# A new timetable for sixteen weight conversions under the attention loop, and shorter zero fills

## The chip, the core and the metric

The kernel runs on one core of a Trainium2 chip. The metric is device time in microseconds (us): the median of three runs is 734.9 us (732.71 to 736.11). The engines are TensorE (PE in the profile, its weight loads PEld), VectorE (DVE), ScalarE (ACT), GpSimd (POOL) and SyncE (SP), which here issues nearly all transfers.

## The reference

Three layers in a row, all in float32 (the last layer's weights arrive as 64-bit floats).

```python
# 1 gated linear attention: q, k, v, f_logit are [4, 8, 768, 48]
f = sigmoid(f_logit)
for t in range(768):
    state = f[t] * state + outer(k[t], v[t])
    y[t] = q[t] @ state
x = y as [3072 tokens, 384]
# 2 mixture of 8 experts, one expert for each token
logits = normed(x) @ normed(expert_emb).T / tau
e = argmax(logits)
x = softmax(logits)[e] * (relu(x @ w1[e]) @ w2[e])      # w1 384x1024, w2 1024x384
# 3 gated layer
out = (((x @ g1) * (x @ g2)) @ w3) @ w_out              # g1, g2 384x1024, w3 1024x1024, w_out 1024x384
```

## The kernel before

**Stages.** Attention is cut into 24 units of 128 time steps (four batches, six chunks of time); a loop of 26 rounds, `for i in range(NU + 2)` at L792, runs them as a software pipeline: in round i the table `parts` (L783) calls each step for unit i minus its own delay. After the loop a hand-written tail ends the routing (which expert takes which token), and the stage of the experts follows, then the last layer. Each token's row is scattered by its rank into `xsd`, 3072 rows of room for each expert; an expert later reads a fixed number of rows (up to 448), so rows that no token fills must hold zeros.

**Conversions.** The last layer's weights come as 64-bit floats. While attention runs, class `Early` (L238) turns sixteen pieces into float32: pieces 0 to 7 are `w_out` (128 rows of 384), 8 to 15 the first four row tiles of `w3` in halves (128 rows of 512). A piece in round u passes `words` (ACT, two reads of `raw`, L263 and L264), `bits` (DVE, L269 and L270), one round later `sums` (POOL, L276), and for `w_out` also `upper` (ACT, L283) and `lower` (POOL, L288). `self.at` (L246) says which round takes which piece: six pieces in seven rounds, in rounds 6 to 11, 13 to 18 and 20 to 23. A piece of `w_out` is 384 KB on its way, one of `w3` 512 KB.

**Loads.** At the end of round i SP is handed the loads of `f_logit` for unit i + 3, of k and q for i + 2 and of v for i (L806 to L809), then a piece's load into one of three `raw` buffers (L810): in round 4 the first three, later always piece k + 3 at the end of the round after piece k's. In rounds 2, 3, 5, 6, 7, 9, 10 and 11 a zero fill of `xsd` follows (L823): rows LO = 256 to 448 of one expert's room. SP takes its list in order, and each transfer waits for the eighth transfer before it.

**Order on the engines.** The schedule is manual: each engine executes in the order in which the calls stand. On ACT `words` stands after the copy of `xl` (L533) and before the copy of `y` (`yT`, L490); a late piece therefore holds up `yT`, whose PSUM bank the transpose `kb` (L466) of the next round takes on TensorE.

**The flag.** `finish_route` (L666) ends with a flag: 1 if an expert's tokens do not fit its window, or if the forget gates are too small. With the flag set, a slow general path is executed after the rest.

Of the kernel before, what the change touches and what calls it, by code (L numbers as in the profile page):

```python
# [7 lines left out]
F32 = mybir.dt.float32  # L8
# [4 lines left out]
ALU = mybir.AluOpType  # L13
AX = mybir.AxisListType
# [5 lines left out]
def attn_moe_glu_kernel(  # L20
# [16 lines left out]
    nc = tc.nc  # L37
    PE, V, A, G, SP = nc.tensor, nc.vector, nc.scalar, nc.gpsimd, nc.sync
# [3 lines left out]
    P = 128  # L42
    NP = H // 2
    NC = S // P
    NU = N // P
# [5 lines left out]
    DENSE = N + CAP  # L51


    LO = 256

    const = ctx.enter_context(tc.tile_pool(name="const", bufs=1))
    dram = ctx.enter_context(tc.tile_pool(name="dram", bufs=1, space=DRAM))
# [2 lines left out]
    def bank(shape, name, tag="ps"):  # L60
        acc = tag == "acc"
        return psum[acc].tile(shape, F32, tag="acc" if acc else "ps", name=name)
# [3 lines left out]
    ones = const.tile([P, P], BF16, name="ones")  # L66
# [11 lines left out]
    flag = const.tile([P, 1], I32, name="flag")  # L78
# [22 lines left out]
    early = pre_pool.enter_context(tc.tile_pool(name="early", side="right", bufs=1, reuse_waits="tile"))  # L101
# [11 lines left out]
        return t.bitcast(F32)  # L113

    RY, RW, RL = 2, 2, 1
    GAP_TILES, BG0, RAW = 4, 6, 3
    FILL = (2, 3, 5, 6, 7, 9, 10, 11)
    PASSES = ((0, 0), (0, 1), (1, 0))

    class Background:  # L120
        def __init__(self):
            self.q = []
# [112 lines left out]
    def w3_piece(i, c):  # L235
        return g3[i * P:(i + 1) * P, c * 512:(c + 1) * 512], 512, "g3", to_w3(i, c)

    class Early:  # L238
# [4 lines left out]
        def __init__(self):  # L243
            self.src = [(go[j * P:(j + 1) * P, :], DM, j) for j in range(KF)]
            self.src += [w3_piece(i, c)[0:2] + ((i, c),) for i in range(GAP_TILES) for c in range(2)]
            self.at = {BG0 + k + k // 6: k for k in range(len(self.src))}  # L246
            self.raw, self.t, self.z = {}, {}, {}

        def load(self, k):
# [154 lines left out]
    fl = lambda t: t.rearrange("p a b -> p (a b)")  # L404

    def s_pre(u):
        for hs in (slice(H // 2, H), slice(0, H // 2)) if u == 0 else (slice(0, H),):
            f = fs[u % NB][:, hs, 0:D]
            A.activation(out=f, in_=f, func=AF.Tanh, scale=0.5)
            if u == 0:  # L410
                A.activation(out=f, in_=f, func=AF.Identity, scale=0.5, bias=half[:, 0:1])
            else:
                G.tensor_scalar(out=f, in0=f, scalar1=0.5, scalar2=0.5, op0=ALU.mult, op1=ALU.add)
# [130 lines left out]
    rt = attn.enter_context(tc.tile_pool(name="rt", reuse_waits="tile", bufs=1))  # L544
# [98 lines left out]
    def choose():  # L643


        b = bank([P, E], "lead", "acc")
        PE.matmul(out=b, lhsT=ones, rhs=base)
        yield
        key, hot, t = [rt.tile([P, E], F32, name=n) for n in ("lkey", "lhot", "lt")]
        s = rt.tile([P, 2], F32, name="ls")  # L650
        V.scalar_tensor_tensor(out=key, in0=b, scalar=float(E), in1=numc, op0=ALU.mult, op1=ALU.subtract)
        yield
        V.tensor_reduce(out=s[:, 0:1], in_=key, axis=AX.X, op=ALU.max)
        yield
        V.tensor_scalar(out=hot, in0=key, scalar1=s[:, 0:1], scalar2=None, op0=ALU.is_equal)
        yield
        V.tensor_tensor(out=t, in0=hot, in1=num, op=ALU.mult)
        V.tensor_scalar(out=hot, in0=hot, scalar1=float(2 * E * N), scalar2=None, op0=ALU.mult)
        yield
        V.tensor_reduce(out=s[:, 1:2], in_=t, axis=AX.X, op=ALU.add)  # L660
        V.tensor_tensor(out=numc, in0=num, in1=hot, op=ALU.subtract)
        yield
        V.tensor_copy(out=first[:, 0:1], in_=s[:, 1:2])
        V.tensor_scalar(out=first[:, 1:2], in0=s[:, 1:2], scalar1=float(N), scalar2=None, op0=ALU.mult)

    def finish_route():  # L666
        okb = rt.tile([P, 1], BF16, name="okb")
        low = rt.tile([P, 1], F32, name="low")
        V.tensor_reduce(out=low, in_=pend.rearrange("p u j -> p (u j)"), axis=AX.X, op=ALU.min)
        V.tensor_scalar(out=okb, in0=low, scalar1=1e-18, scalar2=None, op0=ALU.is_ge)  # L670
        yield
        b, b2 = bank([P, E], "cnt", "acc"), bank([P, 1], "ok", "acc")
        PE.matmul(out=b, lhsT=ones, rhs=base)
        PE.matmul(out=b2, lhsT=ones, rhs=okb)
        yield
        cnt, key, rank, cs, ci, inc, sl = [rt.tile([P, E], F32, name=n) for n in ("cnt", "key", "rank", "cs", "ci", "inc", "sl")]
        gt, hot, t = [rt.tile([P, E, E], F32, name=n) for n in ("cgt", "chot", "ct")]
        fl = rt.tile([P, 2], F32, name="fl")
        big = [P, E, E]
        rows = lambda a: a.unsqueeze(1).to_broadcast(big)  # L680
        cols = lambda a: a.unsqueeze(2).to_broadcast(big)
        V.tensor_tensor(out=cnt, in0=b, in1=cbase, op=ALU.subtract)
        yield
        V.tensor_scalar(out=key, in0=cnt, scalar1=float(E), scalar2=None, op0=ALU.mult)
        yield
        V.tensor_tensor(out=key, in0=key, in1=numc, op=ALU.subtract)
        yield
        V.tensor_tensor(out=gt, in0=rows(key), in1=cols(key), op=ALU.is_gt)
        yield
        V.tensor_reduce(out=rank, in_=gt, axis=AX.X, op=ALU.add)  # L690
        yield
        V.tensor_tensor(out=hot, in0=rows(rank), in1=cols(num), op=ALU.is_equal)
        yield
        V.tensor_tensor(out=t, in0=hot, in1=rows(num), op=ALU.mult)
        V.tensor_tensor(out=hot, in0=hot, in1=rows(cnt), op=ALU.mult)
        yield
        V.tensor_reduce(out=sl, in_=t, axis=AX.X, op=ALU.add)
        V.tensor_reduce(out=cs, in_=hot, axis=AX.X, op=ALU.add)
        yield
        V.tensor_copy(out=slot_e, in_=sl)  # L700
        V.tensor_scalar(out=slot_r, in0=sl, scalar1=float(N), scalar2=None, op0=ALU.mult)
        V.tensor_tensor_scan(out=inc, data0=cs, data1=cs, initial=0.0, op0=ALU.add, op1=ALU.bypass)
        V.tensor_tensor(out=ci, in0=cs, in1=win, op=ALU.subtract)
        V.tensor_tensor(out=offs, in0=inc, in1=cs, op=ALU.subtract)
        V.tensor_reduce(out=fl[:, 0:1], in_=ci, axis=AX.X, op=ALU.max)
        V.tensor_scalar(out=fl[:, 1:2], in0=b2, scalar1=P - 0.5, scalar2=None, op0=ALU.is_lt)
        V.tensor_scalar(out=fl[:, 0:1], in0=fl[:, 0:1], scalar1=0.5, scalar2=None, op0=ALU.is_gt)
        V.tensor_tensor(out=flag, in0=fl[:, 0:1], in1=fl[:, 1:2], op=ALU.add)

    groups = {u0 + n - 1: (u0, n) for u0, n in ((0, 6), (6, 6), (12, 4), (16, 4))}  # L710
    with tc.manual_schedule():
# [45 lines left out]
        def pick_heads():  # L757
            for hb in range(2):
                src = ident[:, 64 * hb:64 * hb + D].unsqueeze(1).to_broadcast([P, NP, D])
                G.tensor_copy(out=sel[:, :, D * hb:D * hb + D], in_=src)  # L760
# [9 lines left out]
        cvt = Early()  # L770
# [16 lines left out]
            (s_out, 3), (s_sq, 4), (cvt.upper, 1), (s_uu, 3),  # L787
        )

        pick_heads()  # L790
        s_pre(0)
        for i in range(NU + 2):  # L792
            for part, late_by in parts:
                if late_by is None:
                    part()
                elif 0 <= i - late_by < NU:
                    part(i - late_by)
            if i == NU - 1:
                spread.append(RL)
            if i == NU - 1:  # L800
                routing.append(choose())
            if i == NU:
                SP.dma_start(out=w1s, in_=phase_src(0, 0, SP))
            if i - 4 in groups:
                routing.append(route(*groups[i - 4]))
            load(f_logit, fs, i + 3)  # L806
            load(k, ks, i + 2)
            load(q, qs, i + 2)
            load(v, vs, i)  # L809
            for n in range(RAW) if i == BG0 - 2 else (cvt.at[i - 1] + RAW,) if i - 1 in cvt.at else ():  # L810
                cvt.load(n)
            if i == 4:
                constants()
            if i == 0:
                warm(8)
                zeros()
            if i in (1, 2, 3):
                step(en)
            if i == 8:
                SP.dma_start(out=idd.rearrange("(p c) w -> p (c w)", c=32), in_=zero[0:DENSE // 32, 0, 0:32].bitcast(I32))  # L820
            if i in FILL:
                e = FILL.index(i)
                SP.dma_start(out=xsd[e * N + LO:e * N + CAP, :].rearrange("(p c) w -> p c w", c=4), in_=zero[0:(CAP - LO) // 4])  # L823
            if i == NU or i == NU + 1:
                step(turn_w[i - NU], 2)
# [345 lines left out]
                V.tensor_copy(out=acc, in_=ob)  # L1171
                SP.dma_start(out=out[bass.ds(r0, P), :], in_=acc)

    with tc.If(nc.values_load(flag[0:1, 0:1], min_val=0, max_val=2) != 0):
        general()


# [28 lines left out]
```

## Time and profile before

| | us |
|---|---|
| median of three runs | 734.9 |
| the profiled execution | 737.25 |
| its span, first to last instruction | 735.5 |
| attention rounds (start to about 150) | about 150 |
| routing's tail, up to the first expert's matmul | 181.09 |
| experts, then the last layer | the rest |

The profiled execution is 2.35 us above the median; 1.75 us of it lie around the span. The page's first part gives each engine's busy time: PE 715.9 us (97%), DVE 348.5, ACT 337.1, POOL 339.7. The mean granted TensorE clock is 0.998 of full speed, the level of 2.4 GHz. In a timeline a row is start, duration, engine, line, operation, output and input, the number of instructions merged in it (x), and in brackets the idle time just before it with what ended it.

### The profile page before, as it was taken

How to read it: one execution, taken by the hardware profiler on the slowest of the kernel's cores; microseconds unless marked ns; L12 is line 12 of the kernel's file. 1: busy time of each engine (PE TensorE's matmuls, PEld its weight loads, DVE VectorE, ACT ScalarE, POOL GpSimd, SP SyncE). 2: the span in 40 equal slices, each digit the busy share in tenths (PEclk: the TensorE clock that was granted, in tenths of full speed). 3: DMA queues.
4: the chain of work that ended last, by engine and by line, in shares of the span. 5: the costliest groups of instructions: out<-in, count | busy, mean ns of one | idle time of the engine just before them, and what ended most of it. 6: DMA issues, size and time to landing. Idle time of an engine off the chain costs nothing.

```text
span 735.5 us, 13353 instructions
## 1 busy us (share of the span) xinstructions
PE 715.9 (97%) x5170; PEld 655.9 (89%) x5170; DVE 348.5 (47%) x682; ACT 337.1 (46%) x703; POOL 339.7 (46%) x423
## 2 busy tenths in 40 slices
PE   8999999989999999999999999999999999999995
PEld 7998989879999999999999988988888888888885
DVE  8889899967556464345343132222322322322322
ACT  5687878755667465465554532122112121121210
POOL 5467787784887676584564952202202201221002
PEclk9999999999999999999999999999999999999999
DMA  9999999742866778644443330000100100100001
GB/s 178 224 216 221 231 238 227 179 174 75 275 205 236 214 238 259 190 148 149 134 141 108 90 85 1 31 13 1 43 1 1 43 1 1 43 1 23 21 1 46
DMA packets 132159, 86.50 MB, mean 118 GB/s; under 512 B 106482, under 2 KB 114682, under 8 KB 132090
## 3 DMA queue, kind: packets, MB, share of 16 engines
q1 hardware_dynamic: 128617, 75.34, 37.9%
q0 software_dynamic: 3072, 9.46, 3.4%
q8 instruction: 42, 0.69, 0.4%
q10 hardware_dynamic: 400, 0.79, 0.3%
q14 instruction: 28, 0.22, 0.1%
HBM read 70.57 MB, written 15.01 MB: 116 GB/s over the span
## 4 chain that ended last, share of the span: by engine, by line
PE 59%; issue 9%; DMA 3%; POOL 2%; ACT 1%; SPq 1%; DVE 0%; POOLq 0%; ACTq 0%; DVEq 0%
PE acc L942 12%; PE hb L928 12%; PE pa L1024 11%; PE pb L1024 10%; PE ob L1037 10%; PE wpb L184 3%; DMA stg<-in_moe_w_dram 2%; DMA gd<-gt 1%; PE xb L915 1%; POOL out_dram L1044 1%; PE w3b L173 0%; POOL x L142 0%; POOL gt L229 0%; ACT wh L141 0%; POOL wl L142 0%
## 5 line engine op out<-in xcount | busy, mean ns | idle before, releaser
L142 POOL TENSOR_TENSOR wl<-stg,wh 128x384 fp32r<-128x384 f32 (+1 forms) x119 | 136.3, 1176 | 57.2 <-ACT wh L141 55.4
L1027 DVE TENSOR_TENSOR a<-a,pb 128x512 f32<-128x512 f32 x48 | 33.0, 687 | 182.0 <-PE pb L1024 175.7
L1037 PE MATMUL ob<-wp,ab 128*128 128x384 f32 x576 | 108.4, 339 | 0.1
L1037 PEld LDWEIGHTS ob<-wp,ab 128*128 128x128 f32 x576 | 102.2, 188 | 4.2 <-DVE ab L1030 0.4
L942 PE MATMUL acc<-h,wh 128*128 128x448 f32 (+7 forms) x384 | 104.2, 351 | 1.4 <-ACT h L930 0.7
L928 PE MATMUL hb<-xT,wh 128*128 128x448 f32 (+7 forms) x384 | 102.4, 348 | 0.0
L1024 PE MATMUL pa<-x,wh 128*128 128x512 f32 x288 | 90.2, 394 | 0.0
L1024 PE MATMUL pb<-x,wh 128*128 128x512 f32 x288 | 89.9, 393 | 0.0
L931 DVE SCALAR_TENSOR_TENSOR h<-hb,h 128x448 fp32r<-128x448 f32 (+7 forms) x64 | 37.0, 578 | 106.0 <-ACT h L930 105.8
L1026 ACT COPY a<-pa 128x512 f32<-128x512 f32 x48 | 28.2, 586 | 120.6 <-PE pa L1024 120.6
L1044 POOL DMA_INDIRECT out_dram<-o,didx x24 | 23.2, 965 | 129.7 <-DVE o L1043 126.3
L142 POOL TENSOR_TENSOR x<-xd,x 128x512 fp32r<-128x512 f32 x18 | 22.8, 1290 | 120.3 <-ACT x L141 120.3
L1029 ACT CAST ab<-a 128x512 fp32r<-128x512 f32 x48 | 29.8, 621 | 104.8 <-DVE a L1027 104.8
L141 ACT CAST wh<-stg 128x384 fp32r<-128x384 f32 (+1 forms) x121 | 61.2, 562 | 29.8 <-DMA stg<-in_moe_w_dram 23.6
L942 PEld LDWEIGHTS acc<-h,wh 128*128 128x128 f32 x384 | 70.4, 188 | 4.8 <-DVE h L931 1.9
L928 PEld LDWEIGHTS hb<-xT,wh 128*128 128x128 f32 x384 | 70.8, 188 | 1.3
L928 PE MATMUL hb<-xT,wl 128*128 128x448 f32 (+7 forms) x192 | 66.7, 347 | 0.0
L942 PE MATMUL acc<-h,wl 128*128 128x448 f32 (+7 forms) x192 | 66.6, 347 | 0.0
L1024 PEld LDWEIGHTS pb<-x,wh 128*128 128x128 f32 x288 | 54.2, 188 | 12.7
L1024 PEld LDWEIGHTS pa<-x,wh 128*128 128x128 f32 x288 | 53.6, 188 | 9.2
L930 ACT ACTIVATE h<-hb 128x448 fp32r<-128x448 f32 (+7 forms) x64 | 32.4, 506 | 62.2 <-PE hb L928 62.1
L1024 PE MATMUL pb<-x,wl 128*128 128x512 f32 x144 | 56.9, 395 | 0.0
(200 smaller groups left out, 1280.7 us busy)
## 6 DMA issues: line engine op xcount, KB each, us to landing
stg<-in_moe_w_dram SPq DMA_DIRECT2D x30, 768.0 KB
raw<-in_moe_w_dram SPq DMA_DIRECT2D x28, 512.0 KB
xs<-xsd SPq DMA_DIRECT2D x8, 675.5 KB
q<-in_q_dram SPq DMA_DIRECT2D x24, 192.0 KB
k<-in_k_dram SPq DMA_DIRECT2D x24, 192.0 KB
v<-in_v_dram SPq DMA_DIRECT2D x24, 192.0 KB
f<-in_f_logit_dram SPq DMA_DIRECT2D x23, 192.0 KB
raw<-in_moe_w_out_dram SPq DMA_DIRECT2D x8, 384.0 KB
```

Of the source, the lines that this page charges most:

```text
L141: A.copy(out=hi, in_=src)
L142: eng.tensor_tensor(out=lo, in0=src, in1=f32(hi), op=ALU.subtract)
L928: PE.matmul(out=b, lhsT=w[x][:, kk, cs], rhs=xT[e][y][:, kk, :], start=(kk + n == 0), stop=(kk == KD - 1 and n == 2))
L930: A.activation(out=h[0], in_=b, func=AF.Relu)
L931: V.scalar_tensor_tensor(out=h[1], in0=b, scalar=0.0, in1=f32(h[0]), op0=ALU.max, op1=ALU.subtract)
L942: PE.matmul(out=acc[d], lhsT=w[x][:, s % 4, d * P:(d + 1) * P], rhs=hs[s][y], start=(s + n == 0), stop=(s == KF - 1 and n == 2))
L1024: PE.matmul(out=b, lhsT=w[x][:, kk, cs], rhs=x2[n][y][:, kk, :], start=(kk + m == 0), stop=(kk == KD - 1 and m == 2))
L1026: A.copy(out=t, in_=pa)
L1027: V.tensor_tensor(out=t, in0=t, in1=pb, op=ALU.mult)
L1029: A.copy(out=ab[s][0], in_=t)
L1037: PE.matmul(out=oacc[t], lhsT=ab[s][x][:, t * P:(t + 1) * P], rhs=wp[:, y, s, :], start=(s + m == 0), stop=(s == KF - 1 and m == 2))
L1044: ins = G.indirect_dma_start(out=out, out_offset=bass.IndirectOffsetOnAxis(ap=didx[:, j:j + 1], axis=0), in_=o, in_offset=None,)
```

## The change

Pieces stand in four of every five rounds, 6 to 9, 11 to 14, 16 to 19 and 21 to 24, so the last falls in round 24, after the last unit's round 23. Two loads are issued in round 4, and later piece k + 2 at the end of the round after piece k's: for the third and fourth piece of each group of four that is the round just before its `words`. The number of `raw` buffers stays three. The zero fills begin at row 320, and the flag is set too if an expert has fewer than 320 tokens.

```diff
-    LO = 256
+    LO = 320
-    GAP_TILES, BG0, RAW = 4, 6, 3
+    GAP_TILES, BG0, RAW, AHEAD = 4, 6, 3, 2
-            self.at = {BG0 + k + k // 6: k for k in range(len(self.src))}
+            self.at = {BG0 + k + k // 4: k for k in range(len(self.src))}
-        fl = rt.tile([P, 2], F32, name="fl")
+        fl = rt.tile([P, 4], F32, name="fl")
...
-        V.tensor_tensor(out=flag, in0=fl[:, 0:1], in1=fl[:, 1:2], op=ALU.add)
+        V.tensor_reduce(out=fl[:, 2:3], in_=cs, axis=AX.X, op=ALU.min)
+        V.tensor_scalar(out=fl[:, 2:3], in0=fl[:, 2:3], scalar1=LO - 0.5, scalar2=None, op0=ALU.is_lt)
+        with nc.allow_low_precision(reason="sums of zeros and ones"):
+            V.tensor_reduce(out=flag, in_=fl[:, 0:3], axis=AX.X, op=ALU.add)
...
+        early = (cvt.words, cvt.bits, cvt.sums, cvt.upper, cvt.lower)
...
-                elif 0 <= i - late_by < NU:
+                elif 0 <= i - late_by < (NU + 2 if part in early else NU):
...
-            for n in range(RAW) if i == BG0 - 2 else (cvt.at[i - 1] + RAW,) if i - 1 in cvt.at else ():
+            for n in range(AHEAD) if i == BG0 - 2 else (cvt.at[i - 1] + AHEAD,) if i - 1 in cvt.at else ():
                 cvt.load(n)
...
-    with tc.If(nc.values_load(flag[0:1, 0:1], min_val=0, max_val=2) != 0):
+    with tc.If(nc.values_load(flag[0:1, 0:1], min_val=0, max_val=3) != 0):
```

SP's list at the end of round 7 and through round 8, before (`raw_818` is piece 3, `raw_926` piece 4):

```order
L386 DMA v3_127<-in_v_dram 128x8x48
L253 DMA raw_818<-in_moe2_w_out_dram 128x768
L823 DMA xsd_83<-wp_91 48x1544
L386 DMA f2_123<-in_f_logit_dram 128x8x48
L386 DMA k1_119<-in_k_dram 128x8x48
L386 DMA q1_116<-in_q_dram 128x8x48
L386 DMA v0_124<-in_v_dram 128x8x48
L253 DMA raw_926<-in_moe2_w_out_dram 128x768
```

The same place of SP's list in the changed kernel, where `raw_816` is piece 2 and `raw_924` piece 3:

```order
L387 DMA v3_127<-in_v_dram 128x8x48
L254 DMA raw_816<-in_moe2_w_out_dram 128x768
L829 DMA xsd_83<-wp_91 32x1544
L387 DMA f2_123<-in_f_logit_dram 128x8x48
L387 DMA k1_119<-in_k_dram 128x8x48
L387 DMA q1_116<-in_q_dram 128x8x48
L387 DMA v0_124<-in_v_dram 128x8x48
L254 DMA raw_924<-in_moe2_w_out_dram 128x768
```

The list has the same shape; each of its places holds an earlier piece, and the fills have 32 partitions for 48.

ACT in round 8, changed kernel: the reads of the piece loaded in the list above at the end of round 7 (before, round 8 reads piece 2, `raw_517`, loaded in round 4, and `raw_818` is read in round 9):

```order
L534 COPY xt_142<-xl_865 128x384
L264 ACTIVATE gt_875<-raw_816 128x384
L265 ACTIVATE z_876<-raw_816 128x384
L526 COPY sbd2_130<-scm2_134 64x4x48 x2
L491 COPY yT_906<-y_889 128x512
```

The piece that SP issues at the end of a round is now read in the next one, ahead of `yT`.

POOL around round 25, before (`am` is the last unit's mask, the DMAs are the scatters of tokens):

```order
L634 DMA xsd_83<-xt_142,pi_2248 24576x386
L641 MEMSET half_71 128x1
L457 AFFINE_SELECT am_2742<-am_2742 128x512 x2
L634 DMA xsd_83<-xt_142,pi_2665 24576x386
L641 MEMSET half_71 128x1
```

The same place in the changed kernel:

```order
L635 DMA xsd_83<-xt_142,pi_2240 24576x386
L642 MEMSET half_71 128x1
L458 AFFINE_SELECT am_2741<-am_2741 128x512 x2
L277 TENSOR_TENSOR g3_2637<-raw_2594,g3_2637 128x512
L635 DMA xsd_83<-xt_142,pi_2662 24576x386
L642 MEMSET half_71 128x1
```

One sum, that of piece 15, now stands among the last units' scatters; its two DVE and two ACT instructions stand in round 24 in the same way.

## Rows read from the trace of the kernel before

**Rows 1.** The page, second part: busy share of the DMA engines, 40 slices.

```profile
DMA  9999999742866778644443330000100100100001
```

**Rows 2.** Timeline, PE: `a` opens rounds 8, 9 and 23.

```profile
40.66 1.16 PE L450 MATMUL a<-qd,kd 64*128 64x128 f32 x16
46.71 1.16 PE L450 MATMUL a<-qd,kd 64*128 64x128 f32 x16
49.17 0.60 PE L466 MATMUL kb<-ident,kd 128*128 128x128 f32 x4
...
135.76 1.16 PE L450 MATMUL a<-qd,kd 64*128 64x128 f32 x16
```

**Rows 3.** Waits of PE, 34 to 136 us: total, times, longest.

```profile
PE kb L466 <- ACT yT L490: 1.9, 5, 0.5
PE xl L532 <- DVE scm L510: 0.5, 1, 0.5
```

**Rows 4.** Timeline, ACT, rounds 8 and 9.

```profile
45.73 0.59 ACT L263 ACTIVATE gt<-raw 128x384 int32<-128x384 uint32 x1 [0.62 <-POOL wo L288]
...
47.39 0.59 ACT L490 COPY yT<-y 128x512 f32<-128x512 f32 x1
...
52.91 0.56 ACT L263 ACTIVATE gt<-raw 128x384 int32<-128x384 uint32 x1 [1.74 <-DMA raw<-in_moe_w_out_dram]
...
54.54 0.59 ACT L490 COPY yT<-y 128x512 f32<-128x512 f32 x1
```

**Rows 5.** Timeline, SP: issues of pieces at the ends of rounds 7 and 17.

```profile
47.88 0.72 SPq L253 DMA_DIRECT2D raw<-in_moe_w_out_dram  x1
...
111.78 0.64 SPq L253 DMA_DIRECT2D raw<-in_moe_w_dram  x1
```

**Rows 6.** Waits of ACT, 30 to 148 us.

```profile
ACT gt L263 <- DMA raw<-in_moe_w_out_dram: 5.9, 4, 1.8
...
ACT g L263 <- DMA raw<-in_moe_w_dram: 4.0, 3, 1.6
```

**Rows 7.** Issues by line; stretches (busy us, clock, DMA share, GB/s).

```profile
raw<-in_moe_w_out_dram SPq DMA_DIRECT2D x8, 384.0 KB
...
xsd<-wp SPq DMA_DIRECT2D x8, 289.5 KB
...
30.00:36.00 6.00, 6.00 (x89) 5.66 (x89) 4.21 (x8) 3.65 (x8) 2.20 (x4) 1.00 1.04 286
...
40.66:58.82 18.16, 18.16 (x292) 17.10 (x288) 15.82 (x31) 15.10 (x37) 11.40 (x17) 1.00 1.00 222
```

**Rows 8.** Timelines, DVE and POOL: one small operation in two rounds, a sum.

```profile
72.88 0.91 DVE L617 TENSOR_TENSOR base<-nb,base 128x8 bf16<-128x8 f32 x1
...
111.97 0.15 DVE L617 TENSOR_TENSOR base<-nb,base 128x8 bf16<-128x8 f32 x1
...
72.74 1.02 POOL L276 TENSOR_TENSOR gt<-raw,gt 128x384 int32<-128x384 int32 x1
```

**Rows 9.** Timelines, POOL, DVE and ACT: rounds 23 to 25 and the tail.

```profile
146.71 1.30 POOL L276 TENSOR_TENSOR g<-raw,g 128x512 int32<-128x512 int32 x1
...
163.89 0.58 POOL L590 TENSOR_TENSOR r<-ssq,half 128x1 f32<-128x1 f32 x1 [1.62 <-ACT sq L538]
...
144.10 0.69 DVE L269 TENSOR_SCALAR raw<-z 128x512 int32<-128x512 int32 x1
...
155.59 1.29 DVE L176 TENSOR_TENSOR w3t<-w3b,w3t 128x512 fp32r<-128x512 f32 x2 [2.68 <-ACT w3t L175]
...
173.10 1.29 DVE L176 TENSOR_TENSOR w3t<-w3b,w3t 128x512 fp32r<-128x512 f32 x2 [0.54 <-ACT w3t L175]
...
140.34 0.72 ACT L263 ACTIVATE g<-raw 128x512 int32<-128x512 uint32 x1
...
147.02 0.58 ACT L490 COPY yT<-y 128x512 f32<-128x512 f32 x1 [0.88 <-PE y L485]
...
162.68 0.48 ACT L533 COPY xt<-xl 128x384 f32<-128x384 f32 x1 [2.53 <-DMA xsd<-xt,pi]
```

## The prediction

> **What bounds the kernel now.** I read the page's slices first, then the PE timeline of the attention rounds, PE's waits, ACT's waits on transfers, SP's issues, and last the timelines of the tail. The slices show the DMA engines full for the first seven slices, some 130 us, and then no more [rows 1]: any byte taken from attention's list is transfer time. But full is not bounding. On TensorE, round 8 opens at 40.66 and round 9 at 46.71, so 6.05 us for a round, without a gap between groups. Fifteen rounds, 8 to 22, take 135.76 - 40.66 = 95.10 us [rows 2], where fifteen of 6.05 are 90.75. So TensorE paces attention, and all that a better timetable could save there is 95.10 - 90.75 = 4.35 us, part of it the routing's own few matmuls. Of PE's named waits most are `kb` waiting for ACT's `yT`, 1.9 us in five times, then 0.5 us for DVE's state [rows 3]. `yT` stands behind `words` on ACT, and `words` waited for pieces of `w_out` 5.9 us and of `w3` 4.0 us [rows 6]. So 9.9 us of late pieces cost TensorE about 2 us. How the rest is swallowed is seen in round 9: ACT waits 1.74 us at 52.91 for a piece and `yT` comes at 54.54 [rows 4], yet PE records no wait of that size [rows 3].
>
> **Loads nearer to their use.** Piece 3 was issued at 47.88 [rows 5], as the last of round 7's list, and landed when ACT's wait ended, 52.91 [rows 4]: 5.03 us from issue to landing, since the transfers before it are still on their way. In the changed kernel that place of the list holds piece 2, and piece 2 is wanted a round earlier, where `words` started at 45.73 [rows 4]. What lies ahead of it has shrunk by one 384 KB load (two in round 4, not three) and by four fills, of rounds 2, 3, 5 and 6, each a third of 289.5 KB = 96.5 KB shorter [rows 7]. At the 286 GB/s of the stretch in which pieces were first loaded, that is 1.37 + 4 x 0.35 = 2.8 us; at the 222 GB/s of the rounds after, 1.77 + 4 x 0.44 = 3.5 us [rows 7]. So piece 2 lands between 49.4 and 50.1, and ACT waits 3.7 to 4.4 us. `yT` of that round ended at 47.39 + 0.59 = 47.98, and the next `kb` began at 49.17 [rows 2, 4]: 1.19 us of it are free. TensorE loses 2.5 to 3.2 us once, in rounds 8 and 9; I take 2.9.
>
> That stall shifts all compute and the transfers go on, so the queue catches up. The next near pieces: piece 6 (round 13) and piece 10 (round 18). At the end of round 17, 111.78 [rows 5], SP issued piece 12; now it issues piece 10 there, with two 512 KB loads fewer ahead (1.83 us each at 286 GB/s) and eight fills (2.8 us) [rows 7]: it lands about 111.8 + 5.0 - 3.7 - 2.8 = 110.3. Round 18 opened about 135.76 - 5 x 6.05 = 105.5, and `words` stands 45.73 - 40.66 = 5.1 us into a round [rows 2, 4]: 110.6, and later by what attention has lost by then. So I expect no second stall of that size, and most of the old waits gone: of the 2.4 us in [rows 3], I take off 2.0. Bounds: nothing gone, and all of the 4.35 us gone.
>
> In sentences apart from the sum: the whole list runs at 222 GB/s, and its bulk are rows of 48 floats, 192 bytes. The Trainium skill (DMA: Bandwidth & Descriptors, Specifications) holds that transfers under 512 bytes are below line rate, and its fit in Anatomy of one DMA charges further bytes at 436 GB/s. By that rule a fill's 96.5 KB with its long rows would save an estimated 0.23 us and the 384 KB load 0.9 us; piece 2 would land near 51.1, TensorE would lose 4.2 us, and the sum would be 737.3. The rows here show 286 GB/s at most, for a mixture.
>
> **Fewer bytes.** All eight fills together save 772 KB, 2.8 to 3.5 us of DMA time. They are worth nothing beyond what is counted above, since TensorE sets the pace and no wait for k, q or v is named in [rows 3].
>
> **One conversion moves past the last unit.** Rounds 6 to 23 hold fifteen pieces for sixteen. On DVE, with two operations of about 0.69 us a piece [rows 9], that frees 1.4 us that TensorE does not wait for. In round 24 the piece adds two ACT reads of 0.72 us, two DVE operations of 0.69 us, and in round 25 a POOL sum of 1.30 us. Behind each stands cover: on POOL the sum pushes back five scatters, and then POOL has 1.62 us idle at 163.89, waiting for ACT; on DVE 2.68 us idle before 155.59; on ACT `yT` waited 0.88 us for PE at 147.02 [rows 9]. Only ACT's 1.4 - 0.9 = 0.5 us comes out, and I take 0.2, for `yT` of the next round waits anyway. If the cover is gone, POOL's 1.3 and ACT's 0.5 us count. From the other side: 2.53 us of ACT's wait at 162.68 is put down to a scatter [rows 9], on the path to the last token's routing; if moved scatters free it, the tail gains up to 1.7 us. Bounds of the tail: -1.7 to +1.8.
>
> **The flag.** Two more small DVE operations and a reduction for an addition, on 8 or 3 values: 0.15 us each at the shortest form of such a row [rows 8], 0.3 us, ahead of an operation that waited 0.54 us for ACT at 173.10 [rows 9]. Nothing; 0.3 us without that cover. SP's read of the flag comes as much later, and only the second expert's weights stand behind it.
>
> **The sum.** Against the profiled execution: 737.25 + 2.9 - 2.0 + 0.2 + 0 = 738.35, that is +1.1 us. The median was 734.9, 2.35 us below the profiled execution, so 736.0. The experts' stage and the last layer start later by the same and are not touched.
>
> **Rivals.**
>
> *Every near piece waits* (slower). Seven more pieces are loaded only a round ahead (3, 6, 7, 10, 11, 14, 15; the last two when the list has run short). If SP cannot run ahead, because the buffer of f for round i + 3 comes free only when TensorE has transposed it in round i, the freed DMA time is lost as idle time, and pieces 6 and 10 land 5 us after issues that do not move: about 6.5 us later than reckoned above. Then each costs what piece 2 costs or a little less, 2.4 us: 734.9 + 2.9 + 2 x 2.4 - 2.0 + 0.2 = 740.8. It decides from the point where ACT's wait exceeds about 1.2 us. For it: the four unit loads and a piece fill most of a round, and landing took 5.03 of 6.05 us. Against it: the DMA engines never rest in those slices [rows 1], so SP is ahead, not behind.
>
> *The first wait is small and the old ones vanish* (faster). If piece 2 lands by 48, its wait costs TensorE some 0.5 us, and the 2.4 us of [rows 3] go, with the tail's 1.7: 734.9 + 0.5 - 2.4 - 1.7 = 731.3; with only half of the tail's, 732.2. For it: a third of the transfers ahead are long rows. Against it: 5.03 us from issue to landing.
>
> *POOL's sum delays the last scatters.* If the scatters and not `xl` hold ACT at 162.68, 1.3 us come out: 737.2 with the rest as forecast.
>
> *DVE meets POOL more often.* A `base` operation of 0.15 us took 0.91 us at 72.88, inside POOL's sum of 72.74 to 73.76 [rows 8]. Round 12, where the first route is on DVE, now has a piece and round 10 has none. If two or three operations stretch so, 1.5 to 2 us of DVE time come in round 13; were DVE late there, 737.5. The Trainium skill (SBUF — State Buffer) describes the port pair that VectorE and GpSimd share as an exclusive lock held for a whole instruction; the stretched row agrees.
>
> *The flag rises.* Counting the reference's tokens for these inputs gives 352 for the smallest expert, above 320; the general path stays off.
>
> **How the numbers follow.** Forecast as summed 0.50, every near piece waits 0.20, first wait small 0.17, POOL 0.08, DVE 0.05. The forecast's own range, from its bounds 2.5 to 3.2, -2.4 to 0 and -0.5 to +0.7, is 734.5 to 738.8. The range that should hold 8 times in 10 reaches into both sides: 731.5 to 740.0. A measurement of this kernel can tell 0.5%, 3.7 us, from no change: faster is below 731.2, slower above 738.6. Slower takes most of the first rival and the forecast's edge, 0.21; faster the good end of the second and some unread gain, 0.14; same 0.65.
>
> **What would show it.** ACT's `words` of round 8 waiting some 4 us on a raw load, and PE's `kb` next to it some 3 us; after that rounds of 6.05 us and less than 1 us of PE waits up to round 23. Wrong: further waits of over 2 us at rounds 9, 13, 14 or 18; or no wait in round 8. In the tail, POOL's idle time before its last power gone from 1.62 to about 0.3 us, and the first expert's matmul within 1 us of where the attention shift puts it.

## The result, and the profile after

The changed kernel takes 738.57 us (median of 22 executions, 736.12 to 742.51) where the kernel before, in turn with it, takes 733.97 us (22, 730.59 to 738.38): a ratio of 1.0061, 95% interval 1.0045 to 1.0076. It is slower by 4.6 us. The forecast was 736.0 us, 1.1 us slower, in a range of 731.5 to 740.0 that holds the result; but "no change" had the largest chance, 0.65. The time is just under its mark of 738.6 us for "slower", while the ratio, 0.61%, is past the 0.5% that the mark stood for.

The two profiled executions hide this: 738.14 us after (span 736.4) against 737.25 before (span 735.5). From the first expert matmul to the end they differ the other way, 550.6 us after and 554.6 before. In the profiles of this study that part, which the change does not touch, takes between 550.6 and 556.3 us. So I read the change up to the first expert matmul, `hb`. Before, then after, from the timeline of PE (TensorE):

```profile
180.93 0.57 PE L928 MATMUL hb<-xT,wh 128*128 128x448 f32 x2
```

```profile
185.80 0.57 PE L934 MATMUL hb<-xT,wh 128*128 128x448 f32 x2
```

That is +4.87 us, near the difference of the medians. In the rows shown, lines of the changed kernel stand one higher than before, and six higher from the zero fills on.

The places are two rounds that no longer take about 6 us (6.05 and 6.44 before). The timeline of PE after, the rounds of pieces 2 and 10 (rows 2 are the same round before):

```profile
47.33 1.16 PE L451 MATMUL a<-qd,kd 64*128 64x128 f32 x16
...
49.35 0.60 PE L402 MATMUL f<-ident,f 128*128 128x128 f32 x4
52.90 0.66 PE L467 MATMUL kb<-ident,kd 128*128 128x128 f32 x4 [2.95 <-ACT yT L491]
53.48 0.94 PE L533 MATMUL xl<-sel,yT 128*64 128x104 f32 x16
54.25 1.75 PE L478 MATMUL y<-qd,sbd 128*64 128x128 f32 x16
55.77 1.93 PE L486 MATMUL y<-am,v 128*64 128x128 f32 x16
57.48 0.80 PE L502 MATMUL uu<-v,kk 128*64 128x48 f32 x16
58.20 1.16 PE L451 MATMUL a<-qd,kd 64*128 64x128 f32 x16
...
113.59 1.16 PE L451 MATMUL a<-qd,kd 64*128 64x128 f32 x16
...
117.38 0.66 PE L467 MATMUL kb<-ident,kd 128*128 128x128 f32 x4 [1.17 <-ACT yT L491]
118.73 1.18 PE L533 MATMUL xl<-sel,yT 128*64 128x104 f32 x16 [0.69 <-DVE scm L511]
119.69 1.93 PE L478 MATMUL y<-qd,sbd 128*64 128x128 f32 x16
121.40 1.68 PE L486 MATMUL y<-am,v 128*64 128x128 f32 x16
...
123.46 1.16 PE L451 MATMUL a<-qd,kd 64*128 64x128 f32 x16
```

Round 9 takes 58.20 - 47.33 = 10.87 us, round 19 takes 123.46 - 113.59 = 9.87. The waits in brackets are only a part: behind them the sixteen-matmul groups of `y`, which take 1.04 us in other rounds, take 1.68 to 1.93. The windows of after (columns: length, busy PE, PEld, DVE, ACT, POOL with counts, granted clock, DMA share, GB/s) say why:

```profile
52.00:58.00 6.00, 5.10 (x66) 4.94 (x66) 4.90 (x11) 5.04 (x13) 3.56 (x5) 0.72 0.95 207
118.00:124.00 6.00, 5.31 (x73) 5.21 (x74) 5.86 (x13) 4.67 (x11) 4.25 (x6) 0.72 0.93 215
```

In both, the granted clock is 0.72 on the mean, a mix of the 2.4 and the 1.2 GHz level; in 120 to 122 us it is 0.50.

ACT's reads answer to rows 4 and 6, SP's issues to rows 5. ACT after, timeline of rounds 8 and 18; then SP, the same pieces' issues:

```profile
50.66 0.55 ACT L264 ACTIVATE gt<-raw 128x384 int32<-128x384 uint32 x1 [4.94 <-DMA raw<-in_moe_w_out_dram]
...
52.26 0.59 ACT L491 COPY yT<-y 128x512 f32<-128x512 f32 x1
...
114.75 0.68 ACT L264 ACTIVATE g<-raw 128x512 int32<-128x512 uint32 x1 [3.17 <-DMA raw<-in_moe_w_dram]
```

```profile
46.14 0.66 SPq L254 DMA_DIRECT2D raw<-in_moe_w_out_dram  x1
...
109.20 0.64 SPq L254 DMA_DIRECT2D raw<-in_moe_w_dram  x1
```

ACT waits 4.94 us for piece 2 and 3.17 us for piece 10. Three summary rows (total, times, longest): waits of PE after (34 to 150 us, where rows 3 have five `kb` waits of at most 0.5), then waits of SP for `f` after and before (both 20 to 140 us):

```profile
PE kb L467 <- ACT yT L491: 5.1, 3, 2.9
```

```profile
SPq L387 <- PE f L402: 11.4, 6, 3.4
```

```profile
SPq L386 <- PE f L401: 0.4, 1, 0.4
```

SP now stands 11.4 us before loads of `f`, since the buffer of `f` for unit i + 3 comes free only when TensorE has transposed `f` in round i; before, that row reads 0.4. SP is handed less and so comes to this bar, and the piece's load stands behind it. That bears on piece 10, not on piece 2: the first of the six waits ends at 60.9 us. Piece 2 is late by its place in the list, behind four loads that took SP from 42.83 to 46.14 us.

The fuller account, from the starts of `a` on TensorE: +0.61 us up to round 8 (a wait for piece 0 in round 7, which the two tries below, with the same list up to there, do not have: 6.05 us there for 7.22 here), +4.82 in round 9, 9.87 - 6.44 = +3.43 in round 19, -3.08 in the other rounds up to 23 (the old waits, gone), -0.91 in the tail; sum +4.87.

### The profile page after: what moved, and what is told of

It reads as the page before. It is cut to its first block, busy times and chain, and to the rows that moved or that the text cites. A ratio compares the mean times of both kernels' runs of the same rounds, so it can differ in the third digit from the quotient of the medians.

```text
span 736.4 us, 13356 instructions
## 1 busy us (share of the span) xinstructions
PE 716.8 (97%) x5170; PEld 660.0 (90%) x5170; DVE 349.9 (48%) x684; ACT 338.3 (46%) x703; POOL 339.9 (46%) x423
## 4 chain that ended last, share of the span: by engine, by line
PE 59%; issue 9%; DMA 3%; POOL 2%; ACT 1%; SPq 1%; DVE 0%; POOLq 0%; ACTq 0%; DVEq 0%
PE acc L948 12%; PE hb L934 12%; PE pa L1030 10%; PE pb L1030 10%; PE ob L1043 10%; PE wpb L185 3%; DMA stg<-in_moe_w_dram 2%; PE xb L921 1%; POOL out_dram L1050 1%; DMA gd<-gt 1%; POOL x L143 0%; PE w3b L174 0%; POOL gt L230 0%; ACT wh L142 0%; POOL wl L143 0%
```

## The experiments

Every run was timed in turn with the kernel before, so ratios are to that kernel. The medians of before differ by chip (733.7 to 736.8 us).

| what differs from before | ratio | 95% interval | first `hb`, us |
|---|---|---|---|
| rows from 320 and flag | 0.9967 | 0.9944 to 0.9990 | 177.28 |
| flag alone | 0.9999 | 0.9979 to 1.0019 | 179.51 |
| timetable alone | 0.9963 | 0.9946 to 0.9981 | 178.98 |
| rows, flag, timetable | 0.9955 | 0.9936 to 0.9975 | 178.11 |
| lead of two alone | 1.0094 | 1.0061 to 1.0126 | 186.22 |
| lead of two, load first | 1.0010 | 0.9989 to 1.0030 | 178.57 |
| all (the changed kernel) | 1.0061 | 1.0045 to 1.0076 | 185.80 |
| all, extra matmuls (first try) | 1.0088 | 1.0055 to 1.0122 | 184.98 |
| all, repeated transposes (second try) | 0.9983 | 0.9960 to 1.0007 | 179.72 |
| all, load first | 0.9938 | 0.9913 to 0.9962 | 177.70 |
| all, lead of three, load first | 0.9962 | 0.9943 to 0.9981 | 174.91 |

The last column is of one execution each; the part behind it varies by 5.7 us, so the ratios decide.

**The lead put back, the rest kept.**

```diff
-    GAP_TILES, BG0, RAW, AHEAD = 4, 6, 3, 2
+    GAP_TILES, BG0, RAW, AHEAD = 4, 6, 3, 3
```

> The changed kernel with the lead alone put back: pieces load three ahead, the new timetable, the filled rows from 320 and the flag stay. Theory A (the lead is what costs: two late pieces, each with a wait on TensorE and a slow stretch behind it): both long rounds on TensorE (10.87 and 9.87 us) come back to about 6.1 to 6.5, the first expert matmul starts near 177 us against 185.80 in the changed kernel and 180.93 before, and the time is 729 to 732 us, faster than before. Theory B (the timetable costs, because conversions now run in other rounds and take buffers or engines at the wrong time): it stays near the changed kernel, 736 to 739 us. Theory C (three pieces ahead in three buffers bring SP's waits on a buffer back, wherever the timetable puts the pieces): about as before, 733 to 735 us.

732.85 us, ratio 0.9955. Rounds 9 and 19 take 6.05 and 6.54 us, and TensorE has no `kb` wait up to round 23. Theory A holds in sign and place, with `hb` at 178.11 for the 177 it named; the time is 0.85 us above its range, on a chip where the kernel before takes 735.48. B and C fall. The lead is worth 1.0061 / 0.9955, so 1.06% or 7.8 us, and the rest of the change gains 3.3.

**The lead alone.**

```diff
+    GAP_TILES, BG0, RAW, AHEAD = 4, 6, 3, 2
...
-            for n in range(RAW) if i == BG0 - 2 else (cvt.at[i - 1] + RAW,) if i - 1 in cvt.at else ():
+            for n in range(AHEAD) if i == BG0 - 2 else (cvt.at[i - 1] + AHEAD,) if i - 1 in cvt.at else ():
```

> The kernel before with the lead alone changed: pieces load two ahead, the old timetable (six units for... seven, as before), rows filled from 256, the old flag. Theory A (the lead costs): a wait of TensorE of 2.5 to 3.5 us at piece 2 with slow matmuls behind it, and at one or two later pieces as well, since the old timetable leaves no more room; 736 to 741 us. Theory B (the timetable costs): 732.5 to 735 us, as before.

743.79 us, ratio 1.0094, slower than theory A said. The wait in round 9 is longer than in the changed kernel, since the fills ahead of piece 2 are the old ones; PE's timeline:

```profile
53.90 1.11 PE L466 MATMUL kb<-ident,kd 128*128 128x128 f32 x4 [4.53 <-ACT yT L490]
54.95 1.66 PE L532 MATMUL xl<-sel,yT 128*64 128x104 f32 x16
56.39 1.50 PE L477 MATMUL y<-qd,sbd 128*64 128x128 f32 x16
57.72 1.04 PE L485 MATMUL y<-am,v 128*64 128x128 f32 x16
```

`kb` takes 1.11 us for 0.60 and `xl` 1.66 for 0.94: the slow stretch is here too, and ends before the second group of `y`.

**Rows and flag alone**, with the old timetable and a lead of three; and **the flag alone**, the same kernel with the fills from 256 again:

```diff
-    LO = 256
+    LO = 320
... (and the flag's lines)
```

```diff
-                SP.dma_start(out=xsd[e * N + LO:e * N + CAP, :]...
+                SP.dma_start(out=xsd[e * N + LO - 64:e * N + CAP, :]...
```

> The kernel before with the filled rows from 320 and the new flag alone; the old timetable and the lead of three. Theory A: the rows' writes are 2 x 8 stretches smaller and lie beside loads that wait for nothing, and the flag's two more vector instructions lie beside TensorE: 733 to 734.5 us, no difference. Rival: the flag's chain is on the path at the end of routing, 735 to 736 us. Rival: the smaller writes take the wait off the piece that lands late in the kernel before (its long wait at piece 3), 731 to 733 us.

> The kernel with rows and flag alone, but its rows filled from 256 again: against before only the flag's two instructions and its threshold differ; against the kernel with rows and flag it writes 0.77 MB more in the same eight transfers. Theory A (bytes: 0.77 MB at the 213 GB/s of these rounds is 3.6 us of transfer time, and that is what went with the rows): the waits of the kernel before are back, the first expert matmul starts near 180.9 us and the time is that of before, ratio 0.999 to 1.001. Rival (the gain of the kernel with rows and flag came from the flag or from another layout of the program): it stays at the lower time, ratio 0.996 to 0.998.

733.25 us, ratio 0.9967, for rows and flag; 0.9999 for the flag alone. Neither clears the 0.5% that a measurement tells, but the first interval excludes 1. The third expectation (smaller writes take the wait off the late pieces) came true in the waits; the time, 733.25, lies in the first one's band of 733 to 734.5, but that stood for "no difference", and the kernel before took 735.48 in turn with it. ACT's wait rows on raw loads, 30 to 150 us, with rows and flag:

```profile
ACT gt L264 <- DMA raw<-in_moe_w_out_dram: 0.3, 1, 0.3
```

In rows 6 they are 5.9 and 4.0 us; with the flag alone they are 3.0 and 4.9 (`hb` at 179.51, 1.4 us earlier than theory A said). So 0.77 MB less to write is worth about 2.4 us by these two ratios, whose intervals overlap, and no cost of the flag is seen.

**The timetable alone**, with a lead of three, rows from 256, the old flag.

```diff
-            self.at = {BG0 + k + k // 6: k for k in range(len(self.src))}
+            self.at = {BG0 + k + k // 4: k for k in range(len(self.src))}
... (and the two lines that let a piece run past the last unit)
```

> The kernel before with the timetable alone changed (five units for four pieces); lead of three, rows from 256, old flag. The prediction's step (the new timetable takes the old waits away, 2.0 us): rounds 10, 11, 16 and 17, which are 6.76, 7.03, 6.83 and 6.95 us in the kernel before, come to 6.05 or 6.46, the first expert matmul starts near 178.5 us and the time is 2 us under before, 733.5 against 735.5. Rival (the waits go with the bytes of the filled rows, since the transfers are busy all through these rounds; the timetable moves nothing): as before, within 1 us, 734.5 to 736.5 us, with waits of about the same sum in other rounds.

733.89 us against 736.79, ratio 0.9963, or 2.7 us faster: the prediction's step, and the rival falls. The four rounds that the expectation calls 10, 11, 16 and 17 are 11, 12, 17 and 18 in the count of this document; they take 6.05, 6.46, 6.22 and 6.46 us. Rows and timetable together give 3.3 us and not 2.4 + 2.7: the same waits can go only once, and with both no wait of ACT on a piece is left between 30 and 150 us.

**Matmuls ahead of the waiting transposes, first try.** Its extra matmuls go into a spare part of a PSUM bank, and there they waited for VectorE's read of that bank: they came behind the wait, not in it.

```diff
+    FILLER = {7: 40, 17: 14}
...
+        for _ in range(FILLER.get(u, 0)):
+            PE.matmul(out=spare[0][:, 192:320], lhsT=ones, rhs=ones)
         kb = bank([P, NP, P], "kb")
...
```

> The changed kernel with 40 extra small matmuls (ones by ones, into columns that nothing reads) ahead of the transposes that wait in the round of piece 2 and 14 ahead of those of piece 10: TensorE works through most of both waits, the waits themselves stay. Theory A1 (the slow stretch behind each wait is TensorE's clock, which falls because the engine stood idle): the granted clock stays at its upper level behind both, the long rounds become about 9.2 and 8.2 us, and the time is 3 us under the changed kernel's, about 735.5 us. Rival A2 (the matmuls behind the wait are slow for what they read or write, or for the burst of transfers then): the slow stretches stay and the time is that of the changed kernel or above it, 738 to 740 us. Rival A3: the extra matmuls outlast the waits and the rounds are as long as before, 738 us, at the upper clock.

742.65 us, ratio 1.0088. As a test of busy waits it failed, but it showed something else. PE's timeline and windows:

```profile
51.92 2.39 PE L468 MATMUL uu<-ones 128*128 128x128 bf16 x40 [3.29 <-DVE scm L516]
54.16 0.61 PE L471 MATMUL kb<-ident,kd 128*128 128x128 f32 x4
...
55.46 1.04 PE L482 MATMUL y<-qd,sbd 128*64 128x128 f32 x16
56.33 1.04 PE L490 MATMUL y<-am,v 128*64 128x128 f32 x16
```

```profile
52.00:58.00 6.00, 6.00 (x112) 5.78 (x113) 4.67 (x9) 4.85 (x13) 4.17 (x6) 1.00 1.14 244
118.00:124.00 6.00, 6.00 (x97) 5.70 (x96) 5.75 (x12) 5.29 (x12) 4.31 (x7) 1.00 0.92 227
```

A wait of 3.29 us, longer than the 2.95 of the changed kernel, and the granted clock stays 1.00 with these 40 small matmuls behind it. They cost 2.24 us and the wait is 0.34 longer; the round grew only from 10.87 to 11.73, so the clock gave back 2.24 + 0.34 - 0.86 = 1.72 us.

**The second try**: the transposes of `f` just ahead of the wait, issued seven times in round 9 and three times in round 19.

```diff
+    AGAIN = {9: 7, 19: 3}
...
-        st["f", u] = [(j[0], j[-1] + 1, tpair(fs[u % NB], "f", "acc", j)) for j in js]
+        st["f", u] = [(j[0], j[-1] + 1, tpair(fs[u % NB], "f", "acc", j, AGAIN.get(u, 1))) for j in js]
```

> The changed kernel with the four transposes of the forget gates, which stand right ahead of the two waits on TensorE, issued seven times in the round of piece 2 and three times in that of piece 10 (the same values written again), so that TensorE works through most of the wait itself; in the run of the first try the extra matmuls waited too and ran behind the wait. Theory A1 (the fall of the granted clock is bound to the idle time): the granted clock stays at its upper level through both rounds, the sixteen-matmul groups behind the waits take 1.04 us each and not 1.75 to 1.93, and the rounds of 10.87 and 9.87 us become about 9.2 and 8.2; the time is 3 us under the changed kernel, ratio to before 1.001 to 1.003. Rival A2 (the matmuls there are slow for another reason, as the burst of transfers): rounds and time as in the changed kernel, ratio 1.006. Rival A3 (the vector engine, which waits for the last of these transposes, is late by them): rounds over 10.5 us at the upper clock, ratio 1.006 or above.

734.83 us, ratio 0.9983 (0.9960 to 1.0007). PE's timeline, and the window behind the wait:

```profile
48.12 3.22 PE L403 MATMUL f<-ident,f 128*128 128x128 f32 x28
51.18 0.62 PE L468 MATMUL kb<-ident,kd 128*128 128x128 f32 x4
51.73 0.94 PE L534 MATMUL xl<-sel,yT 128*64 128x104 f32 x16
52.49 1.04 PE L479 MATMUL y<-qd,sbd 128*64 128x128 f32 x16
53.37 1.04 PE L487 MATMUL y<-am,v 128*64 128x128 f32 x16
```

```profile
52.00:58.00 6.00, 6.00 (x100) 5.65 (x98) 5.16 (x11) 5.30 (x14) 4.12 (x6) 1.00 1.07 213
```

ACT still waits 4.37 us for piece 2, yet TensorE's groups are back to 1.04 us and the round to 8.69 us: A1 holds, A2 and A3 fall. From the start of `kb` to the next `a` the round takes 54.79 - 51.18 = 3.61 us here and 58.20 - 52.90 = 5.30 in the changed kernel: 1.69 us are the clock's. In round 19 of the changed kernel that stretch is 123.46 - 117.38 = 6.08, of which 0.80 is a second wait: 1.67 us again. The gain by the ratios, 0.78% or 5.7 us, is more than the 3 expected. In this execution piece 0 came in time and piece 10 was only 1.93 us late; why the landings fell better is not settled. Round 19 takes 6.97 us, with no wait of TensorE.

**The piece's load first in the unit.** The changed kernel, with the two lines of a piece's load moved ahead of the loads of `f`, k, q and v:

```diff
+            for n in range(AHEAD) if i == BG0 - 2 else (cvt.at[i - 1] + AHEAD,) if i - 1 in cvt.at else ():
+                cvt.load(n)
             load(f_logit, fs, i + 3)
```

> The changed kernel with one edit: in each unit SP issues the piece's load ahead of the unit's four loads of f, k, q and v instead of behind them; the lead stays two. Theory A (a lead of two is short only because SP hangs on the buffers of f and q inside the unit, so the piece's load goes out 3 to 4 us after it could): piece 2 is issued near 42.8 us instead of 46.14 and piece 10 near 105 instead of 109.20, ScalarE's waits on them fall from 4.94 to under 2 and from 3.17 to nothing, TensorE's long rounds come to 6.05 to 6.5, and the time is 731 to 734 us, ratio 0.995 to 0.998. Rival (the transfers are full all through, so whatever goes first delays the rest): piece 2 lands earlier but f, k or q of the next unit land later, TensorE waits for the decay products on VectorE instead, and the ratio is 1.002 to 1.007.

732.27 us, ratio 0.9938 (0.9913 to 0.9962). SP's timeline has pieces 2 and 10 at

```profile
41.29 0.37 SPq L254 DMA_DIRECT2D raw<-in_moe_w_out_dram  x1
...
97.88 0.78 SPq L254 DMA_DIRECT2D raw<-in_moe_w_dram  x1
```

Against the start of their round on TensorE that is 1.48 us after round 8 (39.81) for 4.87 in the changed kernel, and 2.99 us ahead of round 18 (100.87) for 2.07 behind it. ACT's one wait for a raw load is 0.5 us, and rounds 9 and 19 are 6.05 and 6.55: theory A, and beyond its range. The same three stretches on the DMA engines, the changed kernel's first, then this one's, then those of the kernel before:

```profile
60.00:72.00 12.00, 12.00 (x194) 11.31 (x193) 10.88 (x24) 10.27 (x26) 8.71 (x13) 1.00 0.83 205
72.00:85.00 13.00, 13.00 (x206) 12.16 (x205) 12.29 (x31) 10.39 (x27) 8.40 (x12) 1.00 0.95 202
85.00:98.00 13.00, 13.00 (x202) 12.14 (x202) 10.73 (x21) 10.90 (x27) 11.86 (x21) 1.00 0.88 211
```

```profile
60.00:72.00 12.00, 12.00 (x197) 11.16 (x196) 11.12 (x28) 9.15 (x23) 6.63 (x12) 1.00 1.00 225
72.00:85.00 13.00, 13.00 (x203) 12.31 (x201) 12.28 (x27) 11.60 (x30) 10.75 (x16) 1.00 0.99 220
85.00:98.00 13.00, 12.92 (x202) 12.00 (x202) 11.07 (x23) 10.87 (x26) 12.42 (x20) 1.00 1.03 241
```

```profile
60.00:72.00 12.00, 11.13 (x167) 10.02 (x169) 11.25 (x23) 10.06 (x27) 8.36 (x13) 1.00 0.88 221
72.00:85.00 13.00, 12.71 (x208) 11.70 (x202) 12.41 (x31) 10.32 (x27) 9.58 (x16) 1.00 1.02 230
85.00:98.00 13.00, 13.00 (x214) 12.24 (x212) 10.92 (x23) 9.70 (x23) 11.96 (x20) 1.00 0.95 221
```

In the changed kernel SP stands before `f` for 8.1 of its 11.4 us in these 38, and the DMA engines' share is 0.83 to 0.95, where it is 0.99 to 1.03 here and 0.88 to 1.02 before. By the last column that is 12 x 205 + 13 x 202 + 13 x 211 = 7.83 MB against 8.69 here and 8.52 before; a part of the difference is that the kernels do not stand at the same round then and so load other pieces. With the load first, the piece is already out when SP comes to `f`, and the rows for `f` are gone from SP's waits. The lead and the bytes are those of the changed kernel; only the place in SP's list differs. A fourth buffer for `f`, the direct test of the bar, was not run. The Trainium skill (DMA: Bandwidth & Descriptors, Queues, rings and completion order) says that each DMA engine takes the descriptors of one issuer's ring in order, while completions need not come in order; the run fits the first half, in that the piece handed in ahead of four loads is waited for 0.5 us at most; it does not test it on one engine.

**The same on the lead alone** (old timetable, rows from 256), and **the load first with a lead of three**:

> The kernel with the lead alone changed (two ahead, old timetable, rows from 256), and the piece's load issued ahead of the unit's f, k, q and v. Theory A (the lead costs only by the place of the load in SP's list): the 0.9% that the lead alone cost is gone, the waits of 4.5 us go, and the time is that of before or a little less, ratio 0.995 to 1.001. Rival (two ahead is short whenever the transfers are full, as they are with rows from 256; the smaller fills are what made it work in the run with the load first): the ratio stays at 1.004 to 1.009.

> The changed kernel with the load first in the unit and a lead of three: the piece three ahead takes the buffer that the piece of this unit still holds, so SP waits for POOL's sum ahead of the four loads of f, k, q and v. Theory A (SP's position cuts both ways: a lead of three belongs behind the unit's loads, one of two ahead of them): SP waits 2 to 5 us at most pieces, f or q land late, TensorE waits for decay products or transposes, and the ratio is 0.997 to 1.004. Rival (the loads of f, k, q and v have two to three units of slack, so SP may wait): no wait on TensorE, ratio 0.993 to 0.996 as with the lead of two.

Ratio 1.0010 for the first: the 0.9% that the lead cost is gone, as theory A said, and the longest wait of TensorE is 1.28 us. Its piece waits remain, spread out (ACT 8.0 us in six waits for `w3`, 4.3 in two for `w_out`), with no stretch of 2 us below a granted clock of 0.99. Ratio 0.9962 (0.9943 to 0.9981) for the second, 730.82 us: theory A falls and the rival holds, at the edge of its range. SP waits for POOL's sums 2.5 us in two such waits, but f, k, q and v have room. So between two ahead and three ahead no difference is seen once the load goes first; the three versions at 0.9938 to 0.9962 can't be told from one another, and all beat both kernels.

## Why the prediction came out as it did

*Piece 2 late in round 8*: right in kind. It went out at 46.14 and landed when ACT's wait ended, at 50.66, behind the 49.4 to 50.1 of the sum; ACT waited 4.94 us for the 3.7 to 4.4 given. That TensorE's wait, 2.95, met the 2.9 taken is partly luck: attention was 0.61 us late already, by piece 0, so 1.99 us of ACT's wait were covered for the 1.19 reckoned; in the first try, without that delay, TensorE stood 3.29 us. Not in the sum was what follows the wait: 1.69 us at the lower clock level, so the round lost 4.82. This term was mis-sized.

*"So I expect no second stall of that size"*: this step failed. It put piece 10's issue back by the bytes saved ahead of it, 3.7 and 2.8 us, as if SP could always run that far ahead. It went out at 109.20 where piece 12 went at 111.78 before [rows 5], 2.6 us sooner for the 6.5 needed, and came 3.17 us late; with its own clock loss round 19 gave 3.43 us. The cause is the one that the first rival named: SP cannot run ahead for the buffer of `f`. The list of round 17 begins with such a load, from PE's and SP's timelines after:

```profile
102.98 0.60 PE L402 MATMUL f<-ident,f 128*128 128x128 f32 x4
```

```profile
105.01 0.78 SPq L387 DMA_DIRECT2D f<-in_f_logit_dram  x1
```

The buffer came free at 103.58, and from the load of `f` to the piece SP took 109.20 - 105.01 = 4.19 us. So at this pace piece 10 could not have gone out before 103.58 + 4.19 = 107.8, an estimate, where the sum needed 111.78 - 6.5 = 105.3; with the 5.55 us that it then took to land it comes at 113.3, still behind the 111.58 at which ACT wants it. SP's last wait for `f` ahead of it ended at 91.5; how the rest of the delay divides between the bar and the list is not shown.

The rival's second half, that the freed transfer time is lost, is borne out in part: between 60 and 98 us the DMA engines' share is 0.89 for 0.95 before, 0.06 x 38 = 2.3 us of the 6.5 - 2.6 = 3.9 that were missing. Its "against", that the DMA engines never rest [rows 1], was read from slices of 18 us; before, too, the share is 0.88 between 60 and 72 us. The rival was too broad: of the seven further near pieces one cost TensorE a lasting wait; piece 6 did not. The prediction's own signs of being wrong are there: ACT's wait of 3.17 us in round 18, over the 2 us it named, and 1.17 + 0.69 = 1.86 us of TensorE's waits behind the first stall, where it allowed less than 1. A misreading stands beside it: round 18 opened at 104.29 before, not 105.5, which left piece 10 that much less time; attention's own delay gave it back.

*Old waits gone, -2.0*: right in kind, short in size. The timetable alone gave 2.7 us by the ratio; in the changed kernel the other rounds gave 3.08. The range took 2.4 as the most that could go, though the text had just bounded it by 4.35.

*Fewer bytes, worth nothing by themselves*: wrong, as far as a gain below 0.5% can be told. Alone they take away nearly all of ACT's waits on pieces and give 2.4 us. It did not show in the sum because the timetable takes the same waits away.

*The tail and the flag*: within their bounds. POOL's idle time before its last power is gone, as said, and ACT's 2.53 us wait at `xt` is 0.37 (timelines of POOL and ACT after; rows 9 have 1.62 and 2.53 us there):

```profile
168.48 0.60 POOL L591 TENSOR_TENSOR r<-ssq,half 128x1 f32<-128x1 f32 x1
```

```profile
165.78 0.48 ACT L534 COPY xt<-xl 128x384 f32<-128x384 f32 x1 [0.37 <-PE xl L533]
```

In this execution the tail gave 0.91 us back instead of costing 0.2. Why is not shown, and it is no steady gain: from round 23 to `hb` the other runs with the new timetable take 0.4 to 0.7 us more than the 45.17 before (lead put back, timetable alone, first try, load first) or 0.85 and 2.34 less (second try; lead of three, load first). The flag alone measured 0.9999.

The sum with what was measured: 2.95 + 1.69 + 0.18 in round 9, 3.43 in round 19, 0.61 before round 8, -3.08 and -0.91: 4.87, for 1.1 forecast. The missing terms are the clock's loss behind the first stall and the second stall with its own, 1.69 + 3.43 = 5.1 us; the tail and the old waits took 2.2 of it back. So the range holds the result partly by luck: errors of opposite sign that the prediction did not reckon with.

## What to carry to other kernels

A lead counted in rounds is not a lead in time: ask where in the issuing engine's list the load stands and what the entries ahead of it wait for, and try the urgent load at the front before adding buffers or bytes. When a change takes away queued transfers, do not assume that the issuer will run ahead by as much; it stops at the next buffer that compute has to free. Price a stall of TensorE with what follows it at the lower clock, and try each part of a mixed change alone: here two parts gained 3.3 us together and the third cost 7.8.

## What the runs showed of the hardware

In stretches of 2 us the granted clock fell to 0.50 or 0.54 behind waits of TensorE of 2.95 us, of 4.53 us (the lead alone) and of 1.17 plus 0.69 us within one round, and the sixteen-matmul groups of `y` then took 1.50 to 1.93 us for 1.04 (in the lead alone only the first). It did not fall behind a wait of 3.29 us with 40 bf16 matmuls right behind it, nor behind single waits of 0.95 us (round 7 of the changed kernel) and 1.28 us (the lead alone, load first), nor in the kernel before, whose waits between 34 and 136 us are at most 0.5 us. In the changed kernel each fall cost 1.7 us, over half of the 2.95 that the wait itself did. The Trainium skill (TensorE: Matmul & The Clock Gate, Why this matters for your kernels) warns of drops behind idle gaps between matmul bursts; the first two cases agree, the pair of 1.17 and 0.69 us is shorter than the gaps it speaks of, and the wait of 3.29 us without a fall shows that the gap alone does not settle it.
